# Attention, a SiLU MLP and a rational MLP on one core: 64-row matmuls paired on the halves of the array, the output copied into its staging tile, a new order of issue

## The chip, the core and the metric

The kernel runs on one core of a Trainium2 chip: TensorE (PE) multiplies matrices into PSUM, VectorE (DVE), ScalarE (ACT) and GpSimd (POOL) do elementwise work, SyncE (SP) issues the DMAs. Each engine takes its instructions in program order and waits on semaphores for the others. The metric is the device time of one execution in microseconds (us); lower is better.

## The reference

```python
# attention: 2 x 4096 tokens, 192 channels, 8 heads of 24, 7 taps into the past
w = weight_gen - np.max(weight_gen, axis=-1, keepdims=True)
w = np.exp(w)
w = w / (np.sum(w, axis=-1, keepdims=True) + 1e-09)
out = np.einsum('bshk,bskhg->bshg', w, x_unf)      # x_unf: the 7 last tokens
# first MLP, 192 -> 2048 -> 192
h = x @ w_in
g = h * (1.0 / (1.0 + np.exp(-h)))
return (g @ w_out).astype(np.float32)
# second MLP, 192 -> 2048 -> 192
P = a[0] + a[1] * h + a[2] * h2 + a[3] * h3
Q = 1.0 + np.abs(b[0]) * np.abs(h) + np.abs(b[1]) * h2
g = P / (Q + 1e-06)
return (g @ w_out).astype(np.float32)
```

All is float32 in and out, 8192 tokens.

## The kernel before

The tokens go in 16 blocks of 512. A block is turned to channels by tokens (`T`: transposes), passes through eight units of the first MLP (`A0` to `A7` the input product, `C0` to `C7` the output product), is folded and split again (`EC`, `EM`, `XH1`, `XL1`), passes through eight units of the second MLP (`B0` to `B7`, `D0` to `D7`), and is turned back (`FC`, `FT`, `FE`) and stored (`O`). A unit is 256 of the 2048 hidden channels.

A product in full precision is made of rounded ones: each operand is split into a high and a low part (`xh`, `xl`, `wa..`, `wb`, `g1h`, `g1l`, `g2h`, `g2l`), and the matmuls of a unit add high by high, high by low and low by high. The 192 input channels are 128 + 64. The 64 stand twice in the 128 rows of the second half of `xh` and `xl`, and `WB[m]` holds the high part of the last 64 rows of the weights in rows 0 to 63 and the low part in rows 64 to 127, so that one pass of 128 rows makes two products. A unit's input product (`mm1`, line 516) is so 2 x 5 matmuls of 512 columns, one set for each 128 hidden channels; the fifth, `wb` by `xl`, adds high by low in its upper rows and low by low in its lower ones. The output product (`mm2`, lines 537 to 541) is 2 x 5 matmuls too. Input products lie in a tile `h` of two PSUM banks; there are two such tiles, which `T`, `FT` and all units share in turn. `A` units free their tile by `S`, `H` (ACT) and `L` (DVE, line 561); `B` units by `U`, `V` (ACT) and `u`, `w` (DVE, lines 602 and 605).

What follows a `B` unit: `Y`, `N`, `G`, `g` make the quotient, `h0` to `h7` round it (line 217 on POOL, 215 on ACT, 219 on DVE) and `l0` to `l7` take the rest (line 632). The attention of a later block is worked between the units: for each of four token groups a product `M` (line 436), sums `p`, `r`, `a` (lines 445, 449, 455).

Every step is recorded as an operation with a name; a table `KEYS` gives each name a number, and a middle block's number grows by 72 per block. The operations are issued in the order of these numbers, each to its engine, and the table `ENGINES` says which of the allowed engines an operation runs on where it isn't the first. Nothing else decides the order. Buffers are pools with a count (`BUFS`); an operation that takes a buffer waits until the last reader of its former content is done. In the last step of a block, `FC` copies the sums into a tile `of` (one buffer), `FT` turns them back into `h`, `FE` copies that into a tile `o`, and `O` stores `o`. The tile `e` of `EC` is the same buffer as `of`.

The first weights come in 8-byte words and are decoded on ACT and DVE (`weights`) while the first blocks run; three softmax pieces of the later tokens (`s1` to `s3`) are worked on DVE and ACT at the start and in two of the middle blocks.

Of the kernel before, what the change touches and what calls it, by code (L numbers as in the profile page):

```python
# [19 lines left out]
JB = 4  # L20
# [18 lines left out]
    cn:-2654.87 q0O0l:-1091.22 q0O2l:-1019.12 q0O0a:-846.22 q0A0l:-814.6 q0O2a:-791.41 q0A0a:-787.86 q0O01:-777.66  # L39
    q0O02:-773.39 q0O03:-728.14 q0O21:-683.64 q0B0l:-641.23 q0O04:-622.79 q0O22:-558.4 q0B0a:-553.51 q0B01:-551.38  # L40
    q0O0h:-534.54 q0O23:-490.66 q0A01:-489.63 q0O24:-458.65 q0A1l:-456.85 q0A02:-443.96 q0O2h:-432.99 cl:-416.6
    q0A1a:-414.24 s0l:-411.67 q0O0x:-411.37 q0A03:-410.2 s0m:-410.01 q0A04:-404.48 zX:-403.47 q0A0h:-401.08 ca:-383.3
    q0O1l:-377.93 s0e:-364.89 q0A11:-364.45 q0B02:-363.26 q0A0x:-362.65 q0O1a:-361.6 q0A2l:-354.79 q0O2x:-345.81
    q0B03:-316.92 q0A12:-309.71 q0B04:-303.11 s0n:-287.19 q0A2a:-276.83 q0B0d:-276.41 q0O11:-275.19 q0B0h:-271.54
    q0A13:-270.4 zM0:-265.19 q0O12:-257.47 q0A21:-246.3 q0A14:-238.64 zp0:-238.19 q0A22:-237.38 zr0:-229.4
    q0A23:-224.88 za0:-219.64 q0O13:-215.26 zM1:-214.13 q0A24:-200.03 q0O6l:-191.2 q0A3l:-175.29 q0A1h:-175.16
    q0A1x:-172.73 q0A3a:-168.08 zp1:-167.7 q0B1l:-164 q0A31:-160.72 q0O6a:-160.16 zr1:-157.97 q0O61:-156.06
    za1:-153.62 q0O62:-150.5 zM2:-148.24 q0O14:-147.91 zp2:-143.67 q0A32:-141.33 q0A2h:-139.04 zr2:-130.1
    q0B0x:-129.28 X:-122.84 za2:-121.15 q0O1h:-119.09 q0O63:-116.78 q0O3l:-114.33 zM3:-113.33 q0B1a:-108.33
    q0O1x:-107.5 zp3:-105.83 q0A33:-104.78 AW:-103.75 zr3:-103.7 M0:-102 q0B11:-99.99 p0:-99.17 q0O64:-98.62 r0:-95.49  # L50
# [18 lines left out]
    L7:39.16 zL7:39.78 q1O0a:40.59 q1A1a:40.61 q1O01:41.22 q1A11:42.51 C7:42.68 zC6:44.87 q1A12:45.54 zC7:46.34
    zEC:47.04 EC:47.63 q1O02:47.96 EM:48.17 q1A13:48.18 q1B14:49.89 zEM:49.99 q1A33:50.18 q1A14:50.33 q1B1d:50.75  # L70
    XH1:50.98 q1A1h:52.25 zXH1:52.35 q1A1x:53.2 XL1:54.32 zXL1:54.44 zB2:55.99 B2:56.94 zU2:57.59 q1O03:57.63
    q1A34:58.12 q1O04:58.57 q1A3h:58.58 U2:59.61 V2:60.06 zu2:60.2 zV2:60.24 zw2:60.55 u2:60.8 q1O1l:60.82 q1A3x:60.89
    zY2:61.22 w2:61.87 zB0:62.37 B0:63.3 q1B1h:64.35 q1B1x:64.57 q1O1a:64.77 V0:65.24 q1O11:65.24 U0:65.35 Y2:66.19
# [48 lines left out]
    q1O7x:1 r2:1 r3:1 zFE:1 zM0:1 zM1:1 zM2:1 zM3:1 za0:1 za1:1 za2:1 za3:1 zh0:2 zh1:1 zh2:2 zh4:1 zl2:1  # L122
# [604 lines left out]
```

## Time and profile before

| what | value |
|---|---|
| median of 3 runs | 1408.63 us (1406.14 to 1409.71) |
| the profiled execution | 1408.39 us |
| its span, first to last instruction | 1406.6 us |
| mean granted TensorE clock | 0.986 of full speed |
| PE busy | 1247.3 us, 89% |
| DVE busy | 1144.8 us, 81% |
| ACT busy | 1044.6 us, 74% |
| POOL busy | 586.3 us, 42% |

Busy times are sums over all instructions of an engine. A matmul's record is longer than the distance to the next one, since matmuls follow each other before the earlier has ended; PE's cost is therefore read from the distance of starts or from the chain, which counts each step once.

### The profile page before, as it was taken

To read this page: it belongs to the slowest core of one execution; us is meant where nothing else is said; L and a number is where in the kernel's file an instruction comes from. 1 tells how busy PE (TensorE), PEld (TensorE's weight loads), DVE (VectorE), ACT (ScalarE), POOL (GpSimd) and SP (SyncE) were. 2 spreads that over 40 slices of the span, in tenths; PEclk is the share of its full clock that TensorE was granted. 3 is DMA by queue.
4 is the path that set the end of the run, shared out by engine and by line. 5 is a ranking of instruction groups with operands and counts; after the bars stand their busy time and mean duration, and the time that the engine had idled before them with its cause. 6 is when DMAs were issued, how large, how long until landed. Compare 5 with 4: busy or idle time off the path is not lost.

```text
span 1406.6 us, 14510 instructions
## 1 busy us (share of the span) xinstructions
PE 1247.3 (89%) x5472; PEld 1001.1 (71%) x5472; DVE 1144.8 (81%) x1073; ACT 1044.6 (74%) x1000; POOL 586.3 (42%) x328
## 2 busy tenths in 40 slices
PE   0288788999999999999999999999999999999976
PEld 0166566777777777787777777777777778788765
DVE  6788789777798878879797897879687888868695
ACT  3356688777878777787877787787877778788784
POOL 0143234354543445354443535445344554532430
PEclk9989999999999999999999999999999999999998
DMA  6531210101010010101001020101001010000000
GB/s 180 155 104 47 66 38 1 35 0 47 1 59 21 1 47 0 47 1 47 0 7 40 1 79 0 50 1 39 9 1 47 0 44 12 1 15 0 12 0 23
DMA packets 24294, 45.00 MB, mean 32 GB/s; under 512 B 10404, under 2 KB 16674, under 8 KB 24224
## 3 DMA queue, kind: packets, MB, share of 16 engines
q1 hardware_dynamic: 24224, 44.07, 10.5%
q8 instruction: 43, 0.70, 0.2%
q14 instruction: 27, 0.22, 0.1%
HBM read 31.86 MB, written 8.01 MB: 28 GB/s over the span
## 4 chain that ended last, share of the span: by engine, by line
PE 63%; DVE 19%; issue 8%; ACT 7%; DMA 2%; SPq 0%; POOL 0%; DVEq 0%; ACTq 0%; POOLq 0%
PE h L516 33%; PE acc L540 5%; PE acc L537 5%; PE acc L538 5%; PE acc L539 5%; PE acc L541 5%; DVE t L602 5%; DVE t L605 4%; ACT y L596 3%; DVE g1l L561 2%; ACT t L592 2%; DVE y L611 1%; PE acc L577 1%; DMA aw<-wsm 1%; DVE pr L445 1%
## 5 line engine op out<-in xcount | busy, mean ns | idle before, releaser
L516 PE MATMUL h<-xh,wa 128*128 128x512 f32 x1024 | 329.6, 403 | 94.4 <-DVE g1l L561 55.3
L516 PEld LDWEIGHTS h<-xh,wa 128*128 128x128 f32 x1024 | 187.3, 191 | 159.9 <-issue 64.3
L217 POOL TENSOR_SCALAR g2h<-t 128x1024 fp32r<-128x1024 f32 x93 | 119.9, 1289 | 405.7 <-PE acc L539 388.6
L602 DVE TENSOR_TENSOR t<-t,h 128x1024 f32<-128x1024 f32 x128 | 155.4, 1215 | 101.0 <-ACT y L596 48.1
L632 POOL TENSOR_TENSOR g2l<-t,g2h 128x1024 fp32r<-128x1024 f32 x88 | 223.9, 2546 | 22.3 <-ACT g2h L215 14.5
L596 ACT ACTIVATE y<-h,b_sb 128x1024 f32<-128x1024 f32 x128 | 142.5, 1113 | 120.6 <-PE h L516 86.1
L611 DVE SCALAR_TENSOR_TENSOR y<-y,b_sb 128x1024 f32<-128x1024 f32 x128 | 205.2, 1615 | 25.0 <-ACT y L596 24.9
L592 ACT ACTIVATE t<-h,a_sb 128x1024 f32<-128x1024 f32 x128 | 153.9, 1203 | 68.6 <-PE h L516 67.6
L516 PE MATMUL h<-xl,wa 128*128 128x512 f32 x512 | 202.2, 395 | 2.3 <-DVE xl L493 2.3
L561 DVE TENSOR_TENSOR g1l<-h,g1h 128x1024 fp32r<-128x1024 f32 x128 | 156.0, 1219 | 57.4 <-ACT g1h L557 57.3
L516 PE MATMUL h<-xh,wb 128*128 128x512 f32 x512 | 202.3, 395 | 0.0
L516 PE MATMUL h<-xl,wb 128*128 128x512 f32 x512 | 201.5, 394 | 0.0
L622 DVE SCALAR_TENSOR_TENSOR t<-t,a_sb,y 128x1024 f32<-128x1024 f32 x128 | 188.1, 1489 | 2.6 <-ACT y L619 2.5
L436 POOL TENSOR_TENSOR pr<-xw,aw 128x1344 f32<-128x1344 f32 x45 | 139.2, 3093 | 117.9 <-DVE ao L455 117.9
L553 ACT ACTIVATE h<-h 128x1024 f32<-128x1024 f32 x128 | 129.0, 1008 | 62.5 <-PE h L516 59.0
L605 DVE SCALAR_TENSOR_TENSOR t<-t,a_sb,h 128x1024 f32<-128x1024 f32 x128 | 163.7, 1280 | 14.1 <-ACT y L596 9.8
L616 ACT ACTIVATE y<-y,c_sb 128x1024 f32<-128x1024 f32 x128 | 146.6, 1148 | 9.3 <-DVE y L611 8.9
L557 ACT ACTIVATE g1h<-h 128x1024 fp32r<-128x1024 f32 x128 | 130.8, 1023 | 16.7 <-PE acc L539 14.3
L619 ACT ACTIVATE y<-y 128x1024 f32<-128x1024 f32 x128 | 125.9, 1048 | 0.4
L516 PEld LDWEIGHTS h<-xl,wa 128*128 128x128 f32 x512 | 97.5, 190 | 24.7 <-DVE xl L493 3.4
L516 PEld LDWEIGHTS h<-xh,wb 128*128 128x128 f32 x512 | 97.7, 191 | 21.5
L516 PEld LDWEIGHTS h<-xl,wb 128*128 128x128 f32 x512 | 97.4, 190 | 21.3
(97 smaller groups left out, 2303.1 us busy)
## 6 DMA issues: line engine op xcount, KB each, us to landing
xw<-in_x_dram SPq DMA_DIRECT2D x14, 960.0 KB, 5.5
raw<-in_moe_w_out_dram SPq DMA_DIRECT2D x16, 384.0 KB, 3.2
out_dram<-o SPq DMA_DIRECT2D x16, 384.0 KB, 5.8
raw<-in_moe_w_in_dram SPq DMA_DIRECT2D x8, 512.0 KB, 3.9
raw<-in_moe_w_in_dram SPq DMA_DIRECT2D x8, 256.0 KB, 4.3
dup<-dec SPq DMA_DIRECT2D x16, 128.0 KB, 2.3
ao<-ao SPq DMA_DIRECT2D x16, 128.0 KB, 2.4
sm<-in_weight_gen_dram SPq DMA_DIRECT2D x3, 560.0 KB
```

What stands on the lines that cost most here:

```text
L436: e.tensor_tensor(out=p.rearrange("p k (h g) -> p k h g", g=G), in0=st[xw][:, j:j + K, :].rearrange("p k (h g) -> p k h g", g=G), in1=weig ...
L516: pe.matmul(out=h[:, i], lhsT=w[:, f], rhs=xx, start=(n == 0), stop=(n == len(terms) - 1))
L557: act.activation(out=t, in_=st[hb], func=AF.Copy)
L561: dve.tensor_tensor(out=t, in0=st[hb], in1=st[gh].bitcast(F32), op=ALU.subtract)
L592: act.activation(out=q, in_=st[hb], func=AF.Identity, scale=a_sb[:, 3:4], bias=a_sb[:, 2:3])
L596: act.activation(out=q, in_=st[hb], func=AF.Abs, scale=b_sb[:, 1:2])
L602: dve.tensor_tensor(out=st[t], in0=st[t], in1=flat(), op=ALU.mult)
L605: dve.scalar_tensor_tensor(out=st[t], in0=st[t], scalar=a_sb[:, 1:2], in1=flat(), op0=ALU.add, op1=ALU.mult)
L611: dve.scalar_tensor_tensor(out=st[y], in0=st[y], scalar=b_sb[:, 0:1], in1=st[y], op0=ALU.add, op1=ALU.mult)
L616: act.activation(out=st[y], in_=st[y], func=AF.Ln, scale=c_sb[:, 0:1], bias=1e-6)
L622: dve.scalar_tensor_tensor(out=st[t], in0=st[t], scalar=a_sb[:, 0:1], in1=st[y], op0=ALU.add, op1=ALU.mult)
L632: e.tensor_tensor(out=q, in0=st[t], in1=st[gh].bitcast(F32), op=ALU.subtract)
```

## The change

Three things. The fifth matmul of each set loses its low by low half: what is left has 64 rows. For the even set it is the part of `WB[m]` that holds the high weights (`TOP[m]`: rows 0 to 63 for the first MLP, 64 to 127 for the second); for the odd set the same weights are kept in a new tile `WX` in the other 64 rows (`LOW[m]`), written by four new operations `o`. The two 64-row matmuls stand behind the other eight of the unit, on the two halves of the array's rows, with results in the two banks of `h`. `FE` writes back into the tile `of`, `O` stores from there, and the tile `o` is gone. And `KEYS` and `ENGINES` have new numbers.

```diff
-    cn:-2654.87 q0O0l:-1091.22 q0O2l:-1019.12 q0O0a:-846.22 q0A0l:-814.6 q0O2a:-791.41 q0A0a:-787.86 q0O01:-777.66
+    q0O2l:-2483.27 q0O0l:-2341.3 cn:-2221.09 q0O2a:-2105.34 q0O21:-1927 q0O22:-1886.31 q0O23:-1861.3 q0B0l:-1832.2
...
-    h=2, acc0=1, acc1=1, xw=1, aw=2, pr=1, ao=1, xh0=1, xl0=1, xh1=1, xl1=1, of=1, o=1,
+    h=2, acc0=1, acc1=1, xw=1, aw=2, pr=1, ao=1, xh0=1, xl0=1, xh1=1, xl1=1, of=1,
...
+    WX = big.tile([P, NU, P], F32R, name="wx")
+    LOW = [slice(DL, P), slice(0, DL)]
+    TOP = [slice(0, DL), slice(DL, P)]
...
+        def odd(e):
+            w = st[dup][LOW[m]].rearrange("p (u i f) -> p u i f", i=2, f=P)[:, :, 1, :]
+            round_to(e, WX[LOW[m], 4 * c:4 * c + 4, :], w)
...
+        if k == "B":
+            plan.op(name + "o", 0, "ACT POOL DVE", odd, rd=dt, wr=[("WX", m, c)])
...
-                terms = (
-                    (WA[m][0], th[:, 0]),
-                    (WA[m][1], th[:, 0]),
-                    (WB[m], th[:, 1]),
-                    (WA[m][0], tl[:, 0]),
-                    (WB[m], tl[:, 1]),
-                )
+                terms = ((WA[m][0], th[:, 0]), (WA[m][1], th[:, 0]), (WB[m], th[:, 1]), (WA[m][0], tl[:, 0]))
                 for n, (w, xx) in enumerate(terms):
-                    pe.matmul(out=h[:, i], lhsT=w[:, f], rhs=xx, start=(n == 0), stop=(n == len(terms) - 1))
+                    pe.matmul(out=h[:, i], lhsT=w[:, f], rhs=xx, start=(n == 0), stop=False)
+            f = slice(2 * u * P, (2 * u + 1) * P)
+            pe.matmul(out=h[:, 0], lhsT=WB[m][TOP[m], f], rhs=tl[TOP[m], 1], start=False, stop=True)
+            pe.matmul(out=h[:, 1], lhsT=WX[LOW[m], u, :], rhs=tl[LOW[m], 1], start=False, stop=True)
...
         def evac(e):
-            st[o] = t = new("o", [P, JB, D])
+            t = st[of].rearrange("p a c -> p (a c)")[:, 0:JB * D].rearrange("p (j d) -> p j d", d=D)
+            st["o", b] = t
             round_to(e, t, st[tp][:, :, 0:D])
...
-        plan.op("FE", b, "ACT DVE", evac, rd=[(*tp, 0)], wr=[(*o, 0)])
-        plan.op("O", b, "SP", store, rd=[(*o, 0)])
+        plan.op("FE", b, "ACT DVE", evac, rd=[(*tp, 0)], wr=[(*of, 0)])
+        plan.op("O", b, "SP", store, rd=[(*of, 0)])
```

How the new numbers move instructions, at three places of a middle block. First PE, at the end of unit `A6` (`wa_78`, `wb_82` are weights of the first MLP, `wa_80` of the second). Before:

```order
L516 MATMUL h<-xh_3363,wa_78 128x512
L516 MATMUL h<-xh_3363,wa_79 128x512
L516 MATMUL h<-xh_3363,wb_82 128x512
L516 MATMUL h<-xl_3384,wa_78 128x512
L516 MATMUL h<-xl_3384,wb_82 128x512
L516 MATMUL h<-xh_3429,wa_80 128x512
L516 MATMUL h<-xh_3429,wa_81 128x512
L516 MATMUL h<-xh_3429,wb_83 128x512
L516 MATMUL h<-xl_3453,wa_80 128x512
L516 MATMUL h<-xl_3453,wb_83 128x512
```

After:

```order
L525 MATMUL h<-xh_3354,wa_78 128x512
L525 MATMUL h<-xh_3354,wa_79 128x512
L525 MATMUL h<-xh_3354,wb_82 128x512
L525 MATMUL h<-xl_3368,wa_78 128x512
L527 MATMUL h<-xl_3368,wb_82 128x512
L528 MATMUL h<-xl_3368,wx 128x512
L549 MATMUL acc_3487<-g1h,wo_85 128x512
L550 MATMUL acc_3487<-g1h,wo_85 128x512
L551 MATMUL acc_3487<-g1h,wo_85 128x512
L552 MATMUL acc_3487<-g1l,wo_85 128x512
```

The last two rows of the unit are now the pair, and what follows is an output product of the first MLP (`C4`, `acc<-g1h`) where `B4` followed before; `B4` comes ten rows later, and the unit that takes `A6`'s tile, `B6`, comes after `C4`, `B4` and `D0` where it came after `B4` and `D0`.

Second DVE, from the split of a new block (`xl<-tp`) over the copies of the older one to the split of the fold (`xl<-acc`). Before:

```order
L493 TENSOR_TENSOR xl_3384<-tp,xh_3363 128x1024
L219 COPY e<-acc_2951 128x512
L219 COPY o<-to 128x768
L449 TENSOR_TENSOR pr<-pr 128x384
L622 SCALAR_TENSOR_TENSOR t<-t,a_sb,y 128x1024
L455 TENSOR_TENSOR ao<-pr 128x192
L622 SCALAR_TENSOR_TENSOR t<-t,a_sb,y 128x1024
L493 TENSOR_TENSOR xl_3453<-acc_2951,xh_3429 128x1024
```

After:

```order
L508 TENSOR_TENSOR xl_3368<-tp,xh_3354 128x1024
L228 COPY of<-to 128x768
L451 TENSOR_TENSOR pr<-xw,aw 128x1344
L644 TENSOR_TENSOR g2l<-t,g2h 128x1024
L634 SCALAR_TENSOR_TENSOR t<-t,a_sb,y 128x1024
L460 TENSOR_TENSOR pr<-pr 128x576
L228 COPY e<-acc_2938 128x512
L464 TENSOR_TENSOR pr<-pr 128x384
L634 SCALAR_TENSOR_TENSOR t<-t,a_sb,y 128x1024 x2
L470 TENSOR_TENSOR ao<-pr 128x192
L508 TENSOR_TENSOR xl_3462<-acc_2938,xh_3457 128x1024
```

The copy to the staging tile (`FE`) stood behind the copy for the fold (`EC`, `e<-acc`); it now stands ahead of it, with four operations between. `EC` takes the buffer that `FE` has written and `O` stores, so it now waits for a DMA too, which it did not before.

Third POOL. Before, twelve rows out of one block:

```order
L445 TENSOR_TENSOR pr<-pr 128x576
L632 TENSOR_TENSOR g2l<-t,g2h 128x1024
L217 TENSOR_SCALAR g2h<-t 128x1024
L436 TENSOR_TENSOR pr<-xw,aw 128x1344
L632 TENSOR_TENSOR g2l<-t,g2h 128x1024
L449 TENSOR_TENSOR pr<-pr 128x384
L632 TENSOR_TENSOR g2l<-t,g2h 128x1024
L436 TENSOR_TENSOR pr<-xw,aw 128x1344
L217 TENSOR_SCALAR g2h<-t 128x1024
L436 TENSOR_TENSOR pr<-xw,aw 128x1344
L217 TENSOR_SCALAR g2h<-t 128x1024
L449 TENSOR_TENSOR pr<-pr 128x384
```

After, all rows of one block (x3 are three equal ones in a row):

```order
L644 TENSOR_TENSOR g2l<-t,g2h 128x1024 x3
L226 TENSOR_SCALAR g2h<-t 128x1024
L451 TENSOR_TENSOR pr<-xw,aw 128x1344
L226 TENSOR_SCALAR g2h<-t 128x1024
L460 TENSOR_TENSOR pr<-pr 128x576
L644 TENSOR_TENSOR g2l<-t,g2h 128x1024
L226 TENSOR_SCALAR g2h<-t 128x1024 x3
L470 TENSOR_TENSOR ao<-pr 128x192
```

In each middle block two of three products (`pr<-xw,aw`), both sums `pr<-pr 128x384`, two of six rests `g2l` and one of six roundings `g2h` have left POOL; they stand on DVE (rows `L451`, `L464`, `L644` and `L228 CAST g2h` there). DVE's list of the whole program has 1171 instructions where it had 1075, POOL's 232 where it had 333.

## Rows read from the trace of the kernel before

**Rows 1.** The page, part 1: busy time, share of span and instructions by engine.

```profile
PE 1247.3 (89%) x5472; PEld 1001.1 (71%) x5472; DVE 1144.8 (81%) x1073; ACT 1044.6 (74%) x1000; POOL 586.3 (42%) x328
```

**Rows 2.** Busy time in two periods of the steady state: us (x instructions), clock.

```profile
core 0: us, PE busy (x) PEld busy (x) DVE busy (x) ACT busy (x) POOL busy (x), PEclk, DMA share, GB/s
427.20:507.60 80.40, 75.61 (x338) 60.87 (x336) 69.40 (x61) 63.22 (x59) 36.05 (x20) 1.00 0.09 29
507.60:588.00 80.40, 76.73 (x342) 62.01 (x342) 65.74 (x57) 61.92 (x58) 37.33 (x20) 1.00 0.07 21
```

**Rows 3.** Timeline of PE: the fold of blocks 2, 14 and 15.

```profile
286.44 1.02 PE L577 MATMUL acc<-e,fold 128*128 128x512 f32 x2
...
1251.98 1.02 PE L577 MATMUL acc<-e,fold 128*128 128x512 f32 x2
...
1328.33 1.02 PE L577 MATMUL acc<-e,fold 128*128 128x512 f32 x2
```

**Rows 4.** The chain in order of time: start us, us, what.

```profile
520.10 0.87 PE tp L472 x8
...
525.53 0.11 PE to L659
525.64 0.17 PE to L660 x2
...
529.04 0.86 PE acc L577 x2
...
536.71 4.55 PE h L516 x20
```

**Rows 5.** Waits of PE in one period, then its timeline at one.

```profile
PE h L516 <- DVE g1l L561: 2.7, 2, 1.6
PE h L516 <- DVE t L605: 1.0, 2, 0.5
...
507.67 0.70 PE L516 MATMUL h<-xh,wa 128*128 128x512 f32 x2 [1.57 <-DVE g1l L561]
```

**Rows 6.** Groups by line and shape: matmuls and weight loads of the input products.

```profile
L516 PE MATMUL h<-xl,wb 128*128 128x512 f32 x512 | 201.5, 394 | 0.0
...
L516 PEld LDWEIGHTS h<-xl,wb 128*128 128x128 f32 x512 | 97.4, 190 | 21.3
```

**Rows 7.** Groups by line and shape on DVE, POOL and ACT.

```profile
L632 POOL TENSOR_TENSOR g2l<-t,g2h 128x1024 fp32r<-128x1024 f32 x88 | 223.9, 2546 | 22.3 <-ACT g2h L215 14.5 <-DVE g2h L219 4.3 <-PE acc L541 0.8
...
L436 POOL TENSOR_TENSOR pr<-xw,aw 128x1344 f32<-128x1344 f32 x45 | 139.2, 3093 | 117.9 <-DVE ao L455 117.9
...
L449 POOL TENSOR_TENSOR pr<-pr 128x384 f32<-128x384 f32 x32 | 46.2, 1443 | 134.4 <-DVE pr L445 134.3
...
L632 DVE TENSOR_TENSOR g2l<-t,g2h 128x1024 fp32r<-128x1024 f32 x40 | 50.0, 1249 | 0.6 <-POOL g2h L217 0.3
...
L436 DVE TENSOR_TENSOR pr<-xw,aw 128x1344 f32<-128x1344 f32 x19 | 29.5, 1552 | 7.2 <-DMA aw<-wsm 7.2
...
L449 DVE TENSOR_TENSOR pr<-pr 128x384 f32<-128x384 f32 x32 | 17.5, 547 | 0.0
...
L445 DVE TENSOR_TENSOR pr<-pr 128x576 f32<-128x576 f32 x48 | 36.4, 758 | 0.0
...
L219 DVE CAST g2h<-t 128x1024 fp32r<-128x1024 f32 x5 | 3.4, 689 | 0.2
...
L215 ACT ACTIVATE wa<-dec 128x512 fp32r<-128x512 f32 x7 | 4.3, 619 | 1.7 <-DVE dec L347 1.7
```

**Rows 8.** Timelines of POOL and DVE: one DVE operation beside POOL, one alone.

```profile
498.41 3.24 POOL L632 TENSOR_TENSOR g2l<-t,g2h 128x1024 fp32r<-128x1024 f32 x1
...
500.45 2.28 DVE L622 SCALAR_TENSOR_TENSOR t<-t,a_sb,y 128x1024 f32<-128x1024 f32 x1
...
528.64 1.28 DVE L622 SCALAR_TENSOR_TENSOR t<-t,a_sb,y 128x1024 f32<-128x1024 f32 x1
```

**Rows 9.** Timeline of DVE at the fold; issue (ns) and landing (us) of the stores.

```profile
526.70 0.69 DVE L219 COPY e<-acc 128x512 f32<-128x512 f32 x1 [1.78 <-PE to L660]
527.31 0.95 DVE L219 COPY o<-to 128x768 f32<-128x768 f32 x1
...
L667 SPq DMA_DIRECT2D out_dram<-o x16: 332/438/619, 334.3 to 1402.8; - x16
...
DMA to landing us min/median/max: 2.3/5.8/9.6
```

More of the change, by code (lines that the diff above doesn't have):

```diff
@@ L69 @@
[L69 to L73, printed above, removed]
@@ new lines @@
+    q0B03:-1381.55 q0O6l:-1378.43 q0A02:-1372.8 q0O0h:-1359.25 s0l:-1304.97 q0B04:-1277.55 q0O0x:-1229.3
+    q0A1a:-1227.91 q0O2x:-1189.38 q0A11:-1164.91 q0O6a:-1140.86 cl:-1134.45 q0A12:-1131.26 q0A3l:-1105.37
+    q0A03:-1090.04 s0m:-1032.81 q0A04:-1031.12 q0B0d:-1025.84 s0e:-1003.35 q0A13:-975.1 q0A14:-966.51 q0O61:-953.83
+    q0B0o:-950.91 q0A1h:-915.72 s0n:-889.68 q0B0h:-875.58 zX:-861.72 zM0:-841.37 q0A0h:-805.34 q0A3a:-804.24
+    q0O3l:-802.97 q0A31:-799.8 q0O62:-794.77 q0A32:-792.53 q0A1x:-781.38 q0A33:-780.27 q0O3a:-773.19 zp0:-762.28
@@ new lines @@
+    q0O44:-498.06 za1:-489.23 q0O4h:-489.06 q1A0l:-483.83 q0B1d:-481.87 q0A21:-474.14 q1A0a:-464.27 zM2:-460.21
+    q0O14:-456.13 zp2:-455.13 cr:-451.97 q0B1h:-449.18 zr2:-445.82 q0O4x:-444.62 q0O5a:-439.02 q1B0l:-430.96
+    q0A22:-422.06 q1A01:-408.69 za2:-402.62 q0B1o:-394.91 q1A02:-385.42 zM3:-377.85 q0O1h:-373.72 q0O51:-367.62
+    zp3:-367.07 q0A23:-360.28 q1A03:-355.09 q0A24:-348.46 q0A2h:-343.62 zr3:-338.91 q1A04:-336.38 q1B1l:-318.74
+    za3:-316.73 q0O52:-313.98 q0O1x:-313.72 q1B0a:-311.82 q0B1x:-311.36 q1B01:-309.57 q0O53:-302.13 q1B02:-298.62
@@ new lines @@
+    q0O54:-293.57 zAD:-293.15 zT:-281.26 q1B1a:-273.45 q1B03:-272.81 q1A3l:-265.72 q0A2x:-265.08 zXH0:-262.57
+    s1l:-251.44 q0O5h:-249.13 q0O5x:-245.53 q1A3a:-241.75 q1B04:-231.45 zXL0:-230.87 q1A2l:-227.2 q1A31:-222.38
+    s1m:-221.76 q1A32:-212.61 q1B0d:-212.2 q1A0h:-204.06 q1A0x:-203.84 q1A33:-202.87 q1B11:-199.28 s1e:-197.13
+    zA0:-192.82 q1B0o:-190.66 q1A34:-181.9 q0O7l:-177.38 q1B12:-171.04 q0O7a:-169.95 zS0:-169.36 q0O71:-163.14
+    q1B13:-161.1 zA2:-159.95 q1O0l:-153.6 q0O72:-153.22 zH0:-152.3 q1B14:-152.14 X:-137.72 zS2:-133.04 q1A3h:-132.35
@@ new lines @@
+    zC7:41.87 q1O13:42.23 q1A2x:44.92 zEC:45.88 EC:46.64 q1O51:46.67 EM:47.96 zEM:49.35 q1O14:50.04 XH1:51.17
+    zXH1:51.49 zXL1:52.13 XL1:52.21 zB0:52.75 q1O32:54.35 zV0:54.59 q1O52:55.1 q1O1h:55.28 zU0:55.31 q1A1x:55.36
+    zB2:55.47 B2:55.59 zY0:56.08 zU2:56.18 U2:56.22 zu0:56.67 zw0:56.85 u2:57.56 w2:57.75 q1O1x:57.83 q1O33:58.07
+    V2:58.25 zu2:59.06 zN0:59.35 zV2:60.66 zG0:60.77 B0:60.78 zw2:60.89 zg0:61.47 q1O53:61.87 zY2:62.41 U0:62.83
+    V0:63.59 zB1:63.85 Y2:63.88 u0:64.36 w0:64.43 q1O34:64.6 q1O54:65.61 q1O5h:66.26 zh0:67.74 B3:68.21 zU1:68.61
@@ new lines @@
+    er3:1026.53 ea3:1026.86 eAD:1026.97 eT:1044.38 eXH0:1047.16 eXL0:1048.52 eA1:1054.35 eS1:1055.68 eA0:1056.27
+    eH1:1058.39 eL1:1059.36 eS0:1061.62 eH0:1062.02 eL0:1063.37 eA2:1064.21 eC0:1064.41 eS2:1066.32 eH2:1066.93
+    eL2:1067.25 eC1:1068.84 eA3:1071.15 eS3:1072.24 eH3:1073.77 eL3:1077.53 eC2:1083.69 eA4:1089 eC3:1091.61
+    eS4:1092.16 eH4:1093.28 eA6:1094.83 eS6:1096.08 eL4:1096.69 eA5:1096.94 eH6:1097.52 eC4:1098.13 eS5:1099.93
+    eH5:1100.98 eL6:1102.44 eL5:1103.37 eA7:1111.33 eS7:1111.73 eC5:1112.6 eH7:1114.65 eC6:1118.86 eL7:1122.34
@@ new lines @@
+    eC7:1122.42 eEC:1128.07 eEM:1129.43 eXH1:1129.95 eXL1:1131.9 eB2:1132.61 eU2:1133.04 eB0:1136.12 eu2:1139.32
+    eV2:1143.68 eU0:1146.32 ew2:1146.95 eu0:1147.34 eB1:1147.64 eV0:1149.37 eV1:1150.57 ew0:1151.18 eB3:1153.01
+    eY0:1156.91 eU1:1157.72 eu1:1157.77 eN0:1157.88 eU3:1158.44 eY1:1160.62 eN1:1160.67 ew1:1160.94 eu3:1163.04
+    ew3:1163.69 eG0:1167.24 eg0:1180.25 eV3:1182.97 eG1:1185.4 eB4:1188.03 eU4:1189.43 eY3:1193.15 eV4:1197.51
+    eY4:1197.61 eu4:1199.09 eY2:1199.91 eh0:1204.64 eg1:1206.04 eB5:1210.86 eN3:1215.01 ew4:1228.54 eN4:1228.96
@@ new lines @@
+    el0:1230.8 eD0:1232.7 eU5:1233.63 eh1:1235.37 eu5:1238.53 eN2:1253.01 ew5:1259.95 eV5:1260.59 eG2:1267.85
+    eB6:1286.24 eg2:1287.27 eG4:1290.27 eG3:1293.91 eY5:1295.34 eB7:1300.89 eg4:1303.89 el1:1304.62 eD1:1311.98
+    eg3:1312.86 eh2:1313.4 eV6:1324.18 eU7:1328.09 eh3:1329.31 el2:1331.46 eu7:1336.85 eN5:1342.55 eY6:1342.65
+    eV7:1345.81 eY7:1346.62 eG5:1372.46 el3:1376.57 eD2:1410.46 eh4:1412.94 eg5:1418.26 eU6:1418.53 eD3:1432.38
+    el4:1452.48 eN7:1470.14 eD4:1472.19 eN6:1488.98 eh5:1505.82 eu6:1505.95 ew6:1507.99 eG6:1523.41 eG7:1534.58
```

132 lines of the change are left out of this document (53 added, 79 removed).

## Prediction

> **What bounds the kernel now.** I read first the busy shares of the whole span [rows 1]: PE leads with 1247 us, DVE follows with 1145. Shares are averages, so next the stretch that repeats. The folds of blocks 2 and 14 start 965.5 us apart [rows 3], 12 periods of 80.46 us: two thirds of the run is one pattern. In a period [rows 2] PE's records cover 76.7 us of 80.4, at full clock (1.00, the higher level), DVE's 65.7, ACT's 61.9, POOL's 37.3. A matmul's record overlaps the next one's, so what PE must do comes from the chain [rows 4]: twenty matmuls of 512 columns count 4.55 us, 0.227 each. A block has 16 units of 20 of them: 72.6. Its transposes add 0.87, the turn back of the result four times 0.11 + 0.17, that is 1.1, and the fold 0.86. Together 75.5 us, and 80.4 - 75.5 = 4.9 us of a period are waits. The list of waits names them [rows 5]: PE waits for a tile `h`, twice for a `g1l` of line 561 (2.7 us, the longest 1.57) and twice for line 605 (1.0), 3.7 in all; the other 1.2 is the end and start of the matmul pipeline at these four places. So PE is the bound, with 15 us of slack on DVE. The first 286 us and the last 154 are not this pattern.
>
> **The pair of half passes.** A unit loses one pass of ten if the two halves run side by side: 0.227 us, times 16 is 3.63 per block, 58 us for 256 units. No row of this trace shows a 64-row matmul or two at once, so I bound it. Best, the pair costs what one pass costs. Worse, the second half waits for its weights: both halves have loads of their own. A weight load's record is 190 ns long [rows 6], but 64-column matmuls, each with a load of 128 columns, follow each other every 85 ns at line 660 (0.17 for two) [rows 4], so two loads take 0.17 us and fit under a pass of 0.227. If they don't, the second half is late by 0.085 to 0.19 us. Worst, the halves run one after the other, and nothing is gained. I take the first, by the 85 ns row, which is nearest: its matmuls too carry a load each. A last bound lies on the other side: the array could have to run empty when it passes from 128 rows to 64 and back. A pass's record lasts 394 ns [rows 6] and the next starts 227 after it, so emptying it costs about 0.167, twice per unit; I take none of it in the sum, for nothing in the trace shows it, and price it as a rival.
>
> The Trainium skill states such an emptying: its page "TensorEngine Tiling (Array Packing)", section "Key Properties", says that changing the tiling mode drains TensorE, while changing only the tile does not. Its page "TensorE: Matmul & The Clock Gate", Part 3, has tiles of different row groups run at once, about 4 ns apart. By the second alone the 256 pairs save an estimated 57 us, by both together the drains take it all back; no run so far shows either.
>
> **The order on PE.** The longest wait, 1.57 us, is that of `B6` for `A6`'s tile, with two units (`B4`, `D0`) between, that is 4.5 us [rows 5, 4]. In the new order `C4`, `B4` and `D0` lie between, 6.6 us, so this wait goes with the drain around it; I take 1.6 off the 4.9. Other places gain or lose a unit between a tile's uses in about equal number, and I leave their waits as they are.
>
> **Work moved from POOL to DVE.** In each middle block DVE takes two products of 1.55, two sums of 0.55, two rests of 1.25 and one rounding of 0.69 us [rows 7]: 3.10 + 1.09 + 2.50 + 0.69 = 7.4. (The 0.76 us sums of line 445 stay three on DVE.) POOL loses two of 3.09, two of 1.44, two of 2.55 and one of 1.29, 15.5 of its 37.3. DVE is slowed while POOL works: the same operation takes 2.28 us beside a POOL subtraction and 1.28 alone [rows 8]. Counting a period's 57 operations at their lone durations I get 63.9 us, 1.8 below the 65.7 shown; with 15.5 of POOL's 37.3 gone some 0.75 of that comes back (bounds 0 and 1.8). DVE: 65.7 + 7.4 - 0.75 = 72.4 us per period. That is beside PE's work as long as the period is longer; its slack shrinks from 14.7 to about 3. In the two blocks with a softmax piece DVE has 69.4 now [rows 2], 76.1 after; with the same 3 us of slack they take 79.1.
>
> **The staging tile.** `FE` costs the same 0.95 us [rows 9]. New is `EC`'s wait on DVE for the store: behind it stand the sums, quotients and `XL1`, and PE's fold and then `B2` wait for them. The store's time to land is 2.3 to 9.6 us, median 5.8 [rows 9]; in the order before it follows a larger load, in the new one nothing stands just ahead. Cover: the four operations between `FE` and `EC`, 1.55 + 1.25 + 1.28 + 0.76 = 4.84 us [rows 7, 8]. PE has `C7`, `A1` and `D2` in that time, 6.8 us. Landing near the low end costs nothing; at the median, with 0.44 us for the issue [rows 9], `EC` is 1.4 us late. Nearest is the low end, since the store is alone; I take 0.2 per block, bounds 0 and 1.4.
>
> **The start and the end.** Four roundings of 64x512 on ACT cost at most 0.62 each [rows 7], beside its idle time in the start. Up to block 2's split DVE has 321 instructions where it had 305, 16 more at 1.07 us on average [rows 1] is 17 us; PE has 48 units with a pass less, 10.9. Either may decide; I take 0, bounds -11 to +17. At the end, two blocks' units have 7.3 us less on PE, which waits there for chains of DVE and ACT half of the time: -4, bounds 0 and -7.
>
> **The sum.** PE per period: 75.5 - 3.6 + 3.3 of waits + 0.2 = 75.4 us, 5.06 less than 80.46. Twelve periods: -60.7; two with a softmax piece take 79.1, which gives back 2 x 3.7 = 7.4; end -4. Together -57.3. The profiled execution took 1408.39 us, against a median of 1408.63, so the two are one for this purpose: 1408.4 - 57.3 = 1351 us. With the waits left at 4.9 and the store's 1.4 it is 1351 + 14 x 2.8 = about 1390 at worst; with both waits and the start at their best ends about 1325. The likeliest case's own range is 1325 to 1372.
>
> **Rivals.**
> DVE becomes the bound. It must then run with 3 us of idle time where it now has 14.7, in order, with operands from ACT and tiles from PE. If 5 to 7 us stay, the period is 77.4 to 79.4: 1375 to 1398, the two softmax blocks included. For it: DVE's waits now are for ACT and PE results and don't shrink by themselves. Against: with less POOL work its operations are shorter and more even.
> The pair is no pair: halves one after the other give PE 75.5 + 3.5 = 79.0 per period, 12 x 1.46 = 17 us and no more: about 1391. A second half late by its weight load, 0.085 to 0.19 us, gives periods of 76.8 to 78.4: 1368 to 1386.
> The array drains at each change of mode, the case on the other side. At 0.167 a change PE gets 5.3 us per period on top, 71.9 + 5.3 + 3.5 = 80.7: with the start and end about 1412. With the next weight load of 0.19 uncovered as well it is 83.8 per period, about 1450. It decides from 5.06 / 32 = 0.16 us a change on: with less, the kernel is still faster.
> The store's landing at the median, by itself, is 14 x 1.2 = 17 us on the forecast: 1368.
>
> **Chances.** The forecast 0.52, DVE as the bound 0.21, the pair in part or in full one after the other 0.10, the drain 0.14, better than 1325 0.03. A measurement of this kernel can tell 0.3%, 4 us. Faster: all but the drain and a sliver of the pair, 0.84; same: 0.05, from the low end of the drain and the serial pair; slower 0.11. The range 1325 to 1398 holds the forecast, DVE's case and most of the pair's, 0.8.
>
> **What would show it.** Right: the two 64-row matmuls of a unit start within some ns of each other and the next pass about 0.23 us later; folds about 75.4 us apart; `EC` starts without a wait for a DMA; no 1.5 us wait ahead of `B6`; DVE over 90% busy in a period and POOL near 22 us. Wrong: a gap of 0.1 us or more at the first row of the pair or the first after it (drain); the second half starting 0.2 us behind the first (no pair); DVE with 5 us or more of idle time in a period while PE waits for lines 605, 561 or 644 (DVE bound); a wait of `EC` for the store.

## The result: 1429.45 us, 1.5% slower

| | us | ratio to before |
|---|---|---|
| before, beside it on the same chip | 1408.2 | |
| after, median | 1429.45 | 1.015 (1.0131 to 1.017) |
| forecast | 1351, range 1325 to 1398 | |

The forecast was wrong by sign. The time lies where the rival of the draining array was priced, between its 1412 and its 1450. The profile that belongs to these runs fell in an execution at a granted clock of 0.85 (1491.02 us); "after" below is another execution of the same kernel, 1429.79 us with a span of 1428.0 at 0.988.

The page, part 1, of after, against [rows 1]:

```profile
PE 1299.4 (91%) x5472; PEld 933.4 (65%) x5472; DVE 1193.6 (84%) x1169; ACT 1039.4 (73%) x1003; POOL 346.3 (24%) x227
```

Each unit has two 64-row matmuls in place of two full ones, so PE's count stays 5472; its busy time grew by 52 us. A period of after that answers to [rows 2]:

```profile
542.00:623.00 81.00, 79.82 (x342) 57.83 (x342) 69.63 (x64) 61.46 (x59) 19.62 (x12) 1.00 0.06 21
```

The clock is at the higher level as before. POOL fell to 19.6 us (22 forecast), DVE rose to 69.6 (72.4 forecast), with 11 us of the period idle. PE's records cover nearly the whole period. The folds of blocks 2, 14 and 15, against [rows 3]:

```profile
294.54 1.12 PE L589 MATMUL acc<-e,fold 128*128 128x512 f32 x2 [0.41 <-DVE e L228]
...
1275.74 1.02 PE L589 MATMUL acc<-e,fold 128*128 128x512 f32 x2
...
1354.19 1.13 PE L589 MATMUL acc<-e,fold 128*128 128x512 f32 x2 [0.19 <-DVE e L228]
```

Blocks 2 and 14 are 981.2 us apart where they were 965.5; 912.2 was forecast (12 x 75.4 + 7.4). Block 2's fold comes 8.1 us later, and from block 14's fold to the end 152.26 us pass where it was 154.62. So +8.1 + 15.7 - 2.4 = +21.4 us, the whole difference of the spans. The same four numbers for each kernel that was run, from its timeline of folds, show where each one gained or lost (fold to fold; two softmax periods are given where they differ):

| kernel | block 2's fold at | normal period | softmax periods | block 14's fold to the end | span |
|---|---|---|---|---|---|
| before | 286.4 | 80.4 | 81.6 | 154.6 | 1406.6 |
| after | 294.5 | 81.2 | 85.3 | 152.3 | 1428.0 |
| after's order, full passes | 294.9 | 80.5 | 84.9, 85.7 | 152.1 | 1421.3 |
| after's order, nine passes | 289.7 | 79.4 | 84.1 | 150.3 | 1400.4 |
| before's order, nine passes | 280.2 | 78.2 | 79.8, 80.7 | 150.8 | 1371.2 |

What stands around a pair, in after's timeline of PE (start, us, engine, line, operation):

```profile
569.04 0.39 PE L525 MATMUL h<-xl,wa 128*128 128x512 f32 x1
569.36 0.49 PE L527 MATMUL h<-xl,wb 64*128 64x512 f32 x1
569.36 0.49 PE L528 MATMUL h<-xl,wx 64*128 64x512 f32 x1
569.78 0.50 PE L549 MATMUL acc<-g2h,wo 128*128 128x512 f32 x1
570.12 0.40 PE L550 MATMUL acc<-g2h,wo 128*128 128x512 f32 x1
570.35 0.39 PE L551 MATMUL acc<-g2h,wo 128*128 128x512 f32 x1
```

The two halves start in the same 10 ns: they run side by side (a run below tests that). But from the last full pass to the pair it is 0.32 us, from the pair to the next pass 0.42, from that to the one after 0.34, and then 0.23 again. Three plain distances are 3 x 0.227 = 0.68; here they are 1.08. A passage into the 64-row mode and back so costs 0.40 us, and a unit, which saves one pass of 0.227, is 0.17 longer. The place is no exception: of the 192 pairs between block 2's fold and block 14's, 167 have no wait of PE beside them, and at all of these the three distances make 1.08 to 1.10 us. The weight loads at the same place:

```profile
568.82 0.19 PEld L525 LDWEIGHTS h<-xl,wa 128*128 128x128 f32 x1
569.36 0.18 PEld L527 LDWEIGHTS h<-xl,wb 64*128 64x128 f32 x1 [0.35 <-issue]
...
569.78 0.19 PEld L549 LDWEIGHTS acc<-g2h,wo 128*128 128x128 f32 x1 [0.24 <-issue]
```

A load normally runs under the pass before (the one at 568.82 is for the pass at 569.04). At a change of mode it is recorded only at the start of its own matmul, with the loader idle for 0.35 and 0.24 us before. PE's waits in the period from 542.15 to 623.24, against [rows 5]:

```profile
PE acc L589 <- DVE e L228: 0.8, 2, 0.4
PE h L525 <- DVE t L617: 0.6, 2, 0.4
PE h L525 <- DVE g1l L573: 0.2, 1, 0.2
```

The wait of 1.57 us ahead of `B6` is gone. PE is the busier for the pairs and waits less for others. The store of the staging tile, all 16 of them, against [rows 9]:

```profile
L680 SPq DMA_DIRECT2D out_dram<-of x16: 332/338/347, 289.4 to 1424.2; - x16
...
DMA to landing us min/median/max: 2.3/2.3/2.6
```

It lands in 2.3 to 2.6 us. The list of waits has no wait of `EC` for it; what PE's fold waits for is `EC`'s place in DVE's queue, as DVE's timeline shows:

```profile
536.09 0.94 DVE L228 COPY of<-to 128x768 f32<-128x768 f32 x1
536.95 1.54 DVE L451 TENSOR_TENSOR pr<-xw,aw 128x1344 f32<-128x1344 f32 x1
...
540.75 0.74 DVE L460 TENSOR_TENSOR pr<-pr 128x576 f32<-128x576 f32 x1
541.42 0.67 DVE L228 COPY e<-acc 128x512 f32<-128x512 f32 x1
```

`FE`, the four operations and `EC` follow each other without a gap; `EC`'s place costs PE 0.4 us a block, the wait at line 589 above.

### The profile page after: what moved, and what is told of

Read it like the earlier page. It is cut to its first block, busy times and chain, and to the rows that moved or that the text cites. A ratio compares the mean times of both kernels' runs of the same rounds, so it can differ in the third digit from the quotient of the medians.

```text
span 1489.2 us, 14508 instructions
## 1 busy us (share of the span) xinstructions
PE 1385.3 (93%) x5472; PEld 957.9 (64%) x5472; DVE 1192.5 (80%) x1169; ACT 1042.3 (70%) x1003; POOL 351.5 (24%) x227
## 4 chain that ended last, share of the span: by engine, by line
PE 86%; DVE 6%; ACT 5%; DMA 2%; issue 1%; SPq 1%; ACTq 0%; DVEq 0%
PE h L525 34%; PE acc L549 10%; PE acc L552 8%; PE acc L551 8%; PE acc L550 8%; PE acc L553 8%; PE h L527 7%; PE acc L589 1%; PE tp L487 1%; DVE t L614 1%; DVE t L617 1%; DVE y L623 1%; ACT y L608 1%; DMA raw<-in_moe_w_in_dram 1%; PE to L672 1%
## 5 line engine op out<-in xcount | busy, mean ns | idle before, releaser
L525 PE MATMUL h<-xh,wa 128*128 128x512 f32 x1024 | 361.6, 437 | 29.6 <-DVE g1l L573 13.2
L226 POOL TENSOR_SCALAR g2h<-t 128x1024 fp32r<-128x1024 f32 x77 | 93.4, 1213 | 555.6 <-PE acc L551 337.2
L525 PE MATMUL h<-xh,wb 128*128 128x512 f32 x512 | 216.4, 423 | 0.0
L525 PE MATMUL h<-xl,wa 128*128 128x512 f32 x512 | 216.2, 422 | 0.0
L623 DVE SCALAR_TENSOR_TENSOR y<-y,b_sb 128x1024 f32<-128x1024 f32 x128 | 195.8, 1540 | 21.3 <-ACT y L608 20.0
L644 POOL TENSOR_TENSOR g2l<-t,g2h 128x1024 fp32r<-128x1024 f32 x66 | 158.7, 2406 | 171.2 <-ACT g2h L224 140.7
L634 DVE SCALAR_TENSOR_TENSOR t<-t,a_sb,y 128x1024 f32<-128x1024 f32 x128 | 164.6, 1297 | 10.1 <-ACT y L631 10.1
L527 PE MATMUL h<-xl,wb 64*128 64x512 f32 x256 | 128.8, 503 | 0.0
L528 PE MATMUL h<-xl,wx 64*128 64x512 f32 x256 | 128.8, 503 | 0.0
L549 PE MATMUL acc<-g2h,wo 128*128 128x512 f32 x256 | 116.5, 455 | 0.8 <-ACT g2h L224 0.8
```

Of the source, the lines that this page charges most:

```text
L525: pe.matmul(out=h[:, i], lhsT=w[:, f], rhs=xx, start=(n == 0), stop=False)
L527: pe.matmul(out=h[:, 0], lhsT=WB[m][TOP[m], f], rhs=tl[TOP[m], 1], start=False, stop=True)
L549: pe.matmul(out=a[:, 0], lhsT=wh, rhs=th[:, c], start=s, stop=False)
L623: dve.scalar_tensor_tensor(out=st[y], in0=st[y], scalar=b_sb[:, 0:1], in1=st[y], op0=ALU.add, op1=ALU.mult)
L634: dve.scalar_tensor_tensor(out=st[t], in0=st[t], scalar=a_sb[:, 0:1], in1=st[y], op0=ALU.add, op1=ALU.mult)
L644: e.tensor_tensor(out=q, in0=st[t], in1=st[gh].bitcast(F32), op=ALU.subtract)
```

## The experiments

The theory was that the passage costs the time, once for every change between 128-row and 64-row matmuls. Its rivals: the new order loses by itself; the cost belongs to each pair and not to the change; the pair isn't concurrent. Later runs ask why the forecast gain would not have come even from a free pair. Medians stand beside runs of the kernel before on the same chip (1407.6 to 1408.3 us).

**Once more, with a profile.** The changed kernel, no edit.

> The changed kernel once more, unchanged, for a trace at the higher clock. Theory A (mode change: TensorE runs empty when it passes from 128 rows to 64 and back) expects the two 64-row matmuls to start together, the first of them about 0.1 us later than the usual 0.227 us after the pass ahead, and the pass behind them about 0.4 us after them, that is some 0.3 us more per unit than ten starts at 0.227 less one. Theory B (the new order: DVE is the bound and PE waits for it) expects PE idle for 5 us or more in a period. Time about 1429 us.

1429.79 us. Its rows are those above.

**The order alone.** After, with the ten full passes of before (and so without the tile `WX` and its four operations):

```diff
+                    (WB[m], tl[:, 1]),
...
-            pe.matmul(out=h[:, 0], lhsT=WB[m][TOP[m], f], rhs=tl[TOP[m], 1], start=False, stop=True)
-            pe.matmul(out=h[:, 1], lhsT=WX[LOW[m], u, :], rhs=tl[LOW[m], 1], start=False, stop=True)
```

> The changed kernel's order, engines and staging tile with the ten full passes per unit of before. Theory A: the pairs cost 256 x (0.33 - 0.227) = 26 us net, so without them 1403 us, a little below the kernel before. Theory B: the pairs gain up to 58 us that the order loses, so 1450 to 1487 us.

1422.64 us, ratio 1.0097 (1.0074 to 1.012): neither of the two numbers that were expected. Two thirds of the loss is there without a pair, so the passages are not the whole of it: the spans differ by 14.7 us, 8.4 of them up to block 2's fold, 7.3 in the two softmax periods, some 1.5 in the ten others, and 2.5 come back behind block 14's fold. A period of it, and PE's waits in it:

```profile
540.90:621.40 80.50, 77.47 (x343) 61.76 (x343) 69.52 (x64) 61.49 (x59) 20.01 (x12) 1.00 0.07 21
```

```profile
PE h L524 <- DVE t L613: 1.5, 3, 0.6
PE h L524 <- DVE g1l L569: 0.8, 2, 0.6
```

With the fold's and a small one of `FT` there are 3.0 us of named waits where [rows 5] has 3.7: the wait at `B6` went, smaller ones came at other places, and the period is 80.5 as before. In the start PE waits longer for the first attention results; the rows of this kernel and of before, up to block 2's fold:

```profile
PE tp L480 <- DVE ao L463: 60.5, 4, 39.4
```

```profile
PE tp L472 <- DVE ao L455: 42.9, 4, 28.6
```

**Two passages a unit.** The pair is cut in two of 256 columns, the first behind the seventh full pass:

```diff
+                    if i == 1 and n == 3:
+                        pair(0)
...
+            pair(1)
```

> The changed kernel with each pair cut into two pairs of 256 columns, the first behind the seventh full pass, the second at the end: the same columns, one more passage to 64 rows and back in each unit. Theory A: 256 x 0.33 = 84 us more, about 1510 us. Theory B: PE has some us of waits per block to hide it in, at most 20 us more. Theory C (each pair's weight loads lie open, wherever it stands): 256 x 0.17 to 0.25, 45 to 65 us more.

1503.22 us, 1.0678 (1.0655 to 1.07): 73.4 us above the changed kernel, 0.29 for each of 256 added passages, with the same columns. Its timeline of PE:

```profile
581.05 0.39 PE L532 MATMUL h<-xh,wb 128*128 128x512 f32 x1
581.37 0.38 PE L523 MATMUL h<-xl,wb 64*128 64x256 f32 x1
...
581.69 0.49 PE L532 MATMUL h<-xl,wa 128*128 128x512 f32 x1
582.11 0.38 PE L523 MATMUL h<-xl,wb 64*128 64x256 f32 x1
...
582.99 0.39 PE L556 MATMUL acc<-g1h,wo 128*128 128x512 f32 x1
```

From 581.05 to 582.99, with the second pair and two passes of the next product between, it is 1.94 us, where four passes and two halves at 0.227 make 1.14: 0.80 more, twice 0.40.

**Three pairs, one passage.** The two passes of `WB` by `xh` become two pairs, at a unit's end with the third. The kernel leaves out the low weights by high input of the last 64 channels; a second high by high stands in their place.

```diff
-                terms = ((WA[m][0], th[:, 0]), (WA[m][1], th[:, 0]), (WB[m], th[:, 1]), (WA[m][0], tl[:, 0]))
+                terms = ((WA[m][0], th[:, 0]), (WA[m][1], th[:, 0]), (WA[m][0], tl[:, 0]))
...
+            for n, xx in enumerate((th, th, tl)):
```

> The changed kernel with the third pass of each set (WB by xh, 128 rows) replaced by a pair of 64-row passes too, so that three pairs stand in a row at a unit's end: as many passes of PE's time, one passage as before. The low weights by high input of the last 64 channels are left out, and a second high by high stands in their place. Theory A: no change, 1429 us within 10. Theory C: two more pairs per unit with open weight loads, 256 x 2 x 0.17 = 87 us more or above.

1433.26 us, 1.0181 (1.0158 to 1.0204), 3.5 above the changed kernel: four more 64-row matmuls a unit, in place of two full passes, cost nearly nothing. Its timeline (the second of each pair left out):

```profile
567.30 0.39 PE L525 MATMUL h<-xl,wa 128*128 128x512 f32 x1
567.62 0.50 PE L528 MATMUL h<-xh,wb 64*128 64x512 f32 x1
...
567.95 0.39 PE L528 MATMUL h<-xh,wb 64*128 64x512 f32 x1
...
568.19 0.39 PE L528 MATMUL h<-xl,wb 64*128 64x512 f32 x1
...
568.51 0.72 PE L525 MATMUL h<-xh,wa 128*128 128x512 f32 x2
```

Inside the mode a pair follows a pair after 0.24, about a pass's distance. Late are the first matmul behind a change (0.32, so 0.09 more) and the second (0.33, so 0.10); on the way back in after it was 0.34, so 0.11. That is 0.20 a change. In after, where the pair stands alone, the late second and the way back fall into one distance, 0.42. That the cost belongs to the pair falls.

**Both halves on the same 64 rows**, so that they can't run at once:

```diff
-            pe.matmul(out=h[:, 1], lhsT=WX[LOW[m], u, :], rhs=tl[LOW[m], 1], start=False, stop=True)
+            pe.matmul(out=h[:, 1], lhsT=WB[m][TOP[m], slice((2 * u + 1) * P, (2 * u + 2) * P)], rhs=tl[TOP[m], 1], start=False, stop=True)
```

> The changed kernel with both halves of the pair on the same 64 rows (the odd set's weights read from WB instead of WX): same columns, same passage to 64 rows and back, but the halves cannot run side by side. If the pair does run side by side, as its records show, the second half adds 0.227 us per unit, 58 us if nothing hides it, about 1475 to 1487 us. If the records only look so, no change, 1429 us.

1470.27 us, 1.044 (1.0411 to 1.0469), 41 above the changed kernel; the second half starts 0.34 us behind the first. So in the changed kernel the pair does run side by side, and saves its pass. The case of a pair that is no pair falls. The 41 are less than the 58 that 256 passes of 0.227 would make, on which the expected 1475 to 1487 us stood.

**Nine full passes**, in after's order and in before's. The kernel leaves out the odd set's fifth pass, the low input of the last 64 channels. PE then has what the forecast gave it, a pair at the price of one pass:

```diff
+                terms = terms[:5 - i]
```

> The new order with nine full passes per unit: PE's time as the forecast had it, with no passage to 64 rows. Left out is the low input by high weight of the last 64 channels for the odd sets. If the mode change is the only step that failed, the forecast's sum holds: about 1351 us, periods of 75.4 us. If the order fails too (DVE at over 69 us of work per period, block 2 eight us late, the softmax periods five us longer), PE cannot use the time: periods of 77.5 us or more, 1385 to 1400 us.

> The kernel before with nine full passes per unit, in its own order; left out is the same product as in the other nine-pass run. If PE is the bound as the forecast read it, 3.63 us less per block with the same waits: 1408 - 12 x 3.6 - 6 = about 1358 us. If the waits for the tiles h (chains of ACT and DVE) grow as PE gets faster, half of it: 1375 to 1390 us.

In after's order 1405.13 us, 0.998 (0.9968 to 0.9992); in before's 1375.24, 0.9766 (0.9743 to 0.9788). A free pair would have brought 3 us in the order of the changed kernel and 33 in the old one, not 57. In after's order the period is 79.4 us for 71.9 of PE's work. Its waits of PE in one:

```profile
PE h L525 <- DVE t L614: 2.5, 3, 1.1
PE h L525 <- DVE g1l L570: 1.3, 2, 0.9
```

and a piece of the chain in it, in order of time:

```profile
566.67 2.66 ACT y L628 x3
...
569.53 1.19 ACT t L601
570.72 0.94 ACT y L628
571.66 1.01 ACT y L605
...
572.70 1.22 DVE t L611
573.92 1.20 DVE t L631
575.12 1.19 DVE t L614
...
576.78 1.14 DVE of L227
577.91 1.14 DVE g1l L570
...
579.19 2.31 PE h L525 x9
```

What releases PE is a chain of 12 us through ACT and DVE: line 628, for the quotients of other units, ahead of lines 601 and 605 on ACT, then the copy of line 227 and others ahead of line 570 on DVE. A shorter PE only waits longer at its end.

**The engines of before for the middle blocks**, in after's order with full passes: the table `ENGINES` has before's entries for the middle blocks (`M1`, `M3`, `h0`, `h1`, `h2`, `h5`, `l3`, `l4`, `p0`, `p1`, `r2` and `r3` differ), all else of the order is after's.

> The new order with ten full passes, and in the middle blocks the engines of the kernel before: POOL has the products, sums, rests and roundings again that the change gave to DVE. If DVE's load is what the order loses by, the softmax periods fall back from 84.9 to about 80.5 us and the whole to about 1410 us. If the order itself loses, 1420 us or more, since POOL's operations take twice as long in places found for DVE.

1486.55 us, 1.0564 (1.0537 to 1.059), the period 85.4: 64 us more than the same order with its own engines. The order and its engines so belong together, and how much of the order's loss is the work moved to DVE stays unknown.

**Less elementwise work.** The sums `p` and `r` of the attention are left out (five of its seven taps), with ten full passes, in after's order and in before's:

```diff
-            plan.op(f"p{j}", b, "DVE POOL", add0, rd=pt, wr=pt)
-            plan.op(f"r{j}", b, "DVE POOL", add1, rd=pt, wr=pt)
```

> The new order with ten full passes, and without the sums p and r of the attention (five of the seven taps are left out): DVE has about 4.4 us less per middle block, POOL 1.5, PE the same work. If DVE's queue is what the new order waits for, the periods fall from 80.5 towards PE's 75.5 plus 2, the whole from 1422 to 1375 to 1390 us. If chains of ACT and PE set the period, at most 10 us less.

> The kernel before without the same sums: DVE has about 3.4 us less per middle block, POOL 3.0, PE the same work. With 15 us of slack on DVE the old order should gain little: 1395 to 1405 us. As large a fall as in the new order would say that DVE was as much the bound before.

1399.1 us, 0.9939 (0.9924 to 0.9954), against 1422.64 with the sums: -23.5. And 1389.09, 0.9868 (0.9854 to 0.9881): -18.5. Block 2's fold comes 5.7 and 11.1 us earlier, and the normal periods are 79.1 and 79.5, 1.4 and 0.9 less. A period of the first:

```profile
530.83:609.90 79.07, 76.97 (x344) 61.90 (x343) 64.23 (x57) 61.49 (x59) 19.75 (x11) 1.00 0.07 21
```

DVE has 5.3 us less to do than with the sums (64.2 against 69.5) and the period is only 1.4 shorter. With -23.5 the first lies between what the two theories expected. DVE is no single bound either; both orders gain alike, so the run doesn't tell DVE's queue from the other waits as the reason for the order's loss.

**Pairs in the old order**, in units 0 and 1 of each MLP, 64 of 256; more, beside the tile `o`, was not tried:

```diff
-                )
+                )[:4 if u < 2 else 5]
...
+            if u < 2:
+                f = slice(2 * u * P, (2 * u + 1) * P)
+                pe.matmul(out=h[:, 0], lhsT=WB[m][TOP[m], f], rhs=tl[TOP[m], 1], start=False, stop=True)
+                pe.matmul(out=h[:, 1], lhsT=WX[LOW[m], u, :], rhs=tl[LOW[m], 1], start=False, stop=True)
```

> The kernel before, in its order and with its tile o, with pairs in the units 0 and 1 of both MLPs (64 of 256 units; more of WX does not fit beside o). By the mode change, 0.40 us against 0.227 saved, each pair costs 0.17 us net: 64 x 0.17 = 11 us more, 1419, or some 1413 if half of it lies in PE's waits. If pairs pay in the old order, 64 x 0.227 = 14 us less, 1394.

1417.39 us, 1.007 (1.0056 to 1.0084): 9.8 us lost, 0.15 a pair, nearly the whole 0.17 by which after's timeline makes a unit longer (at 42 of these 64 pairs the three distances are 1.08 to 1.10 too). A pair loses in an order that has nothing to do with the new one.

**The new end alone.** Before, with after's numbers in `KEYS` and entries in `ENGINES` for the last block's operations (the names that begin with `e`).

> The kernel before with the new numbers for the last block alone (ten full passes, its tile o). The stretch behind block 14's fold takes 152.1 us in the new order with full passes and 154.6 in the old one. If that difference is the last block's order, about 1406 us; if it is what the blocks ahead left over, 1408 us or more.

1440.9 us, 1.0238 (1.0222 to 1.0254): the last three stretches from fold to fold are 83.5, 86.0 and 95.9 us, where before has 80.3, 78.9 and 76.3. Behind the old middle the new end loses 33 us, and what it gives behind the new one this run doesn't show. No version that computes everything beat the kernel before.

## Why the prediction failed, step by step

**"I take none of it in the sum": the step that sets the sign.** The drain of the array, bounded at 0.167 a change and priced as a rival, is 0.20 a change, above the 0.16 from which the prediction said it decides. The bound came from the right rows [rows 6]; wrong was to prefer zero because no row showed it, though the trace had no change of mode in which one could. Shown by three runs: the cost doubles with the passages, stays with three pairs in one, and comes in the old order too. It sets the sign here, since in the same order a free pair, the nine passes, is 3 us (0.2%) faster than before. The order is a loss of its own, though: with full passes, 14 us. The Trainium skill, "TensorEngine Tiling (Array Packing)", section "Key Properties", says that a change of tiling mode drains TensorE, without a price. The traces fit that, with 0.40 us for the way in and back, but don't prove the drain. The Trainium skill's page "TensorE: Matmul & The Clock Gate", Part 3, has row groups side by side some ns apart. The traces agree (0 to 10 ns), and it is of no use at a price of 0.40 for a pass of 0.227. Whether the array empties or the loads just can't go ahead of a change isn't told apart: the records show both at once, and an open load of 0.18 to 0.19 us would make nearly the 0.20 of a change by itself.

**"So PE is the bound": the step that would have failed with a free pair too.** The forecast turned each us of PE's work into a us of time. PE's work a period (75.5 before; less 3.6 with nine passes; plus 6.4 for 32 changes of 0.20) against the measured periods:

| kernel | PE's work | period | the rest: waits |
|---|---|---|---|
| after's order, nine passes | 71.9 | 79.4 | 7.5 |
| after's order, full passes | 75.5 | 80.5 | 5.0 |
| after | 78.3 | 81.2 | 2.9 |
| before's order, nine passes | 71.9 | 78.2 | 6.3 |
| before | 75.5 | 80.4 | 4.9 |

The forecast took the waits as fixed, but they are what is left: where PE works 3.6 us less, the period falls by 1.1 in the new order, 2.2 in the old. PE, ACT and DVE hand two tiles `h` round, and by the waits that grow with nine passes that loop is nearly as long as PE's work. Of the miss of 78 us, 24 come from the passages (1429.5 - 1405.1), of 256 x 0.40 = 102 us that PE spends on them; the rest falls into waits that it had anyway. The other 54 are missing with a free pair too (1405.1 measured, 1351 forecast; 48 of them in the twelve periods, 960.5 against 912.2). Of these, 40 are PE's time that turned into waits (nine passes bring 17.5 us in the new order, of 57) and 14 the order's own loss; counted from the old order it is 24 (33 of 57) and 30. The two act together, and the shares depend on which is taken first. That the rival's sum, with 0.20 put in (1412 + 512 x 0.033 = 1429), gives the measured time holds for a PE this full: its 2.9 us of waits are near the 3.5 assumed.

**"I take 1.6 off the 4.9."** The wait at `B6` did go; the order alone has 5.0 us of waits all the same. A named wait was counted as a gain without asking what is late next.

**The softmax periods and the start.** The surcharge of the softmax periods is about 4.2 us over normal ones, with 3.7 forecast; in the old order it was 1.2. The surcharge comes out nearly right by luck: DVE has 76.0 us of work in them, as forecast (76.1), but it idles for 9.3 us, not 3. The start was taken at 0 with bounds to +17; it is +8.1, by longer waits for the first attention results. What in the new order's front and softmax pieces makes it so is not settled: no run changed them alone.

**Right.** The pair's halves run side by side. DVE did not become the bound in the changed kernel: 69.6 us of 81. For a free pair that rival's signs are there: with nine passes the period is 79.4 us (its range was 77.4 to 79.4), DVE idles for 10 us, and PE waits for lines 614 and 570, the rival's 605 and 561 under other numbers. But the chain there runs through ACT as well. That DVE has 69.6 us and not 72.4 comes from a misreading in the forecast: its 1.8 us of slowdown is a sum of durations set against busy time, in which records that overlap count once. Added up, a period's DVE records exceed the same operations' shortest durations by 5.6 us before and 3.0 after, so 2.5 came back where 0.75 was taken. POOL fell as worked out. The store costs nothing (bounds 0 to 1.4; `EC`'s place costs 0.4, 0.2 was taken). The end gave 2.4 us (4 forecast, bounds 0 to 7), but not for the forecast's reason, the passes saved: the order with full passes gives 2.5.

## What to carry to other kernels

Put 64-row matmuls in long runs or not at all: a way in and back costs 0.40 us here, so one pair for one saved pass of 0.227 loses. By these numbers, as an estimate, it pays from two saved passes on (0.45), which was not run. Before a saved us on the busiest engine is booked, leave the work out in a run (here one line): nine passes would have said 3 to 33 us instead of 57. An order of issue belongs to its assignment of engines; the two mixes that were run took 1441 and 1487 us.

## What the runs showed that was not expected

The second matmul behind a change of mode is late too, and by more (0.10 to 0.11 us) than the first (0.09), on the way in and on the way back. This half of the price is not the mode's alone, and the trace of before already had it: behind a wait of PE, where the loads don't go ahead either, the second matmul comes late in the same way. At the wait of [rows 5] the load goes on record with its matmul:

```profile
507.64 0.30 PEld L516 LDWEIGHTS h<-xh,wa 128*128 128x128 f32 x2 [1.97 <-issue]
...
508.21 0.40 PE L516 MATMUL h<-xh,wb 128*128 128x512 f32 x1
```

From 507.67 to 508.21 two distances take 0.54 us where plain ones take 0.45. At the 48 waits of this kind between block 2's fold and block 14's the second matmul starts 0.31 to 0.34 us behind the first, that is 0.08 to 0.11 late.

And DVE's time is not the sum of its work: without five sums, before's period has 52 DVE instructions instead of 57 and 66.2 us of busy time instead of 65.7. The eight operations of one form in a period take 1908 ns where they took 1694:

```profile
L609 DVE SCALAR_TENSOR_TENSOR y<-y,b_sb 128x1024 f32<-128x1024 f32 x8 | 15.1, 1908 | 1.1 <-ACT y L594 1.1
```

```profile
L611 DVE SCALAR_TENSOR_TENSOR y<-y,b_sb 128x1024 f32<-128x1024 f32 x8 | 13.5, 1694 | 1.5 <-ACT y L596 1.5
```

They don't lie beside POOL more: the share of their time that does is 0.54 with the sums left out and 0.53 before. What moved is which of two starts first. Before, the third of the eight starts 0.23 us ahead of a product on POOL and takes 1.27 us, as the three of the eight do that lie beside nothing on POOL (1.28):

```profile
478.02 1.27 DVE L611 SCALAR_TENSOR_TENSOR y<-y,b_sb 128x1024 f32<-128x1024 f32 x1
...
478.25 3.47 POOL L436 TENSOR_TENSOR pr<-xw,aw 128x1344 f32<-128x1344 f32 x1 [4.22 <-DVE ao L455]
```

Without the sums it starts 0.08 us behind the product, and takes 3.57:

```profile
542.98 2.57 POOL L436 TENSOR_TENSOR pr<-xw,aw 128x1344 f32<-128x1344 f32 x1 [1.76 <-DVE ao L455]
...
543.06 3.57 DVE L609 SCALAR_TENSOR_TENSOR y<-y,b_sb 128x1024 f32<-128x1024 f32 x1 [0.23 <-ACT y L594]
```

It ends 1.08 us behind POOL's operation, and so does the slow one of [rows 8]. No run was made to test this.
